# Attention over a sliding window of a cache, with both projections: the first weight chunks 4 and 5 as two loads, and V of unit 30 as one

## The chip, the cores and the metric

The kernel runs on one core of a Trainium2 chip. The metric is the time of one execution on the device in microseconds (us). TensorE (PE in the profile) does the matmuls and transposes, with its weight loads shown apart as PEld; VectorE is DVE, ScalarE is ACT, GpSimd is POOL, and SyncE (SP) issues the DMA transfers.

## What is computed

Eight sequences of 32 new tokens each (256 rows) are projected to queries of 32 heads, attend over the last 2048 positions of a given cache of K and V with 4 heads, each shared by 8 query heads, and are projected back.

```python
def reference(x, k_cache, v_cache, wq, wo):
    B, Sq, D = x.shape                      # 8, 32, 1024
    Hq, Dh = 32, 128
    Hkv, Sk = k_cache.shape[1], k_cache.shape[2]   # 4, 8192
    W = min(4096, max(256, Sk // 4))        # 2048
    rep = Hq // Hkv                         # 8
    q = (x @ wq).reshape(B, Sq, Hq, Dh).transpose(0, 2, 1, 3)
    k = jnp.repeat(k_cache[:, :, Sk - W:, :], rep, axis=1)
    v = jnp.repeat(v_cache[:, :, Sk - W:, :], rep, axis=1)
    scores = jnp.einsum("bhqd,bhkd->bhqk", q, k) * (Dh ** -0.5)
    p = softmax(scores)
    o = jnp.einsum("bhqk,bhkd->bhqd", p, v)
    return o.transpose(0, 2, 1, 3).reshape(B, Sq, Hq * Dh) @ wo
```

All data are bf16; sums are kept in fp32.

## The kernel before

The work is cut into 32 **units**, one for each pair of a sequence and a K/V head; units 0 to 7 belong to head group 0, and so on. A unit has 2048 keys in 16 tiles of 128, and 256 columns of queries (8 heads of 32 tokens). `run` walks through the units in four slots each. A slot computes the scores of four key tiles on TensorE (L504), has ScalarE take their exponential (L506), and issues, two slots late, the product with V (L515). V is first copied into a buffer `va` with a column of ones beside it (`va_copy`, L437 and L439), so that the product also gives the sum of the exponentials; `finish_unit` divides by it (L445 to L451).

The scores want K with its 128 channels on the partitions, and it comes there in three ways. Units 0, 1 and 2 are loaded plain and transposed on TensorE (L397 for unit 0, L244 for 1 and 2). Units 4, 7, 9 and some later ones are loaded plain, transposed in blocks on VectorE (L259) and moved into place by VectorE and GpSimd (L268, L270). All others are transposed by the DMA itself, in two halves (L200).

The projection of the queries is done by group: a group's part of Wq has 1024 columns, and its 1024 rows come as eight **chunks** of 128 (256 KB each), numbered 0 to 7. For group 0 this is done in `start`, before the first scores: for each chunk, eight matmuls (L405), one for each head. Ahead of chunk 6 stand the eight transposes of the first half of unit 0's K (`k_turn(0)`), after chunk 7 those of the second half. Then the query sums are cast (`q_copy`, L411) and the first scores follow. The later groups' queries (L285) and the output projection (L322) are spread over the slots of the attention by a plan written out by hand.

Nearly all loads are issued by SP, in the order in which the code calls them, and no engine changes its order of work at run time. In `start` this order is: the first half of x (the second is issued by ScalarE), the chunks of Wq up to 5, the first half of K of unit 0, chunks 6 and 7, the second half of that K, V of unit 0 and K of unit 1, and then V of unit 1 and K of units 2 and 4, V of unit 2 and unit 3. `load_wq` takes a tuple `cuts` that says how many chunks each load of a half holds. In this kernel chunks 4 and 5 are one load. Each half has one buffer, whichever way it is cut.

`load_v` brings a unit's V in one load of 512 KB, or in two of 256 KB where the unit's number is at least `V_HALVES`. A unit's `va_copy` reads the whole of it in one instruction either way.

A load tells of its landing through one of eight semaphores that all loads take in turn, whichever engine issues them. A load waits, before it is issued, for the landing of the one that had its semaphore last, which is the load eight places earlier. Loads wait for a free buffer too, where theirs was in use.

Of the kernel before, what the change touches and what calls it, by code (L numbers as in the profile page):

```python
# [17 lines left out]
RL_MIN = 1.0e-10  # L18
N_WARM = 8
VA_ROW = 160  # L20
V_HALVES = 30

PE_T = (0, 1, 2)

# [84 lines left out]
class Fast:  # L109
# [93 lines left out]
    def load_v(self, ui, eng):  # L203
        b, g = self.units[ui]
        self.v_sb[ui] = self.vp.tile([self.P, self.KT, self.Dh], BF16, name="v_sb", tag="v")
        n = self.KT // (2 if ui >= V_HALVES else 1)
        for j in range(0, self.KT, n):
# [131 lines left out]
    def start(self):  # L339
# [6 lines left out]

        nc.sync.dma_start(out=x_sb[:, 0, :], in_=xf[0:P, :])  # L347
        nc.scalar.dma_start(out=x_sb[:, 1, :], in_=xf[P:2 * P, :])
        wq0 = self.load_wq(0, 0, (1, 1, 1, 1)) + self.load_wq(0, 1, (2, 1, 1))
        for p in wq0[:5]:  # L350
            p()
        self.load_k(0, 0)
        wq0[5]()
        wq0[6]()
        self.load_k(0, 1)
        self.load_v(0, nc.sync)
        self.load_k(1)
# [336 lines left out]
```

## Time and profile before

| what | us |
|---|---|
| median of 6 runs | 184.62 (184.25 to 185.02) |
| the profiled execution: its time | 185.06 |
| the profiled execution: its span | 183.3 |
| TensorE busy in the span | 177.3 |
| ScalarE busy | 135.9 |
| VectorE busy | 126.5 |
| GpSimd busy | 89.1 |
| TensorE busy from 0 to 20 us | 17.65 |
| mean granted TensorE clock | 0.998 |

The span runs from the first to the last instruction of the program; the execution's time has some more around it. The page puts the span into 40 slices and gives each engine's busy share in tenths:

```profile
PE   7979999999999999999999999999999999999993
DVE  0218799689887699477799566777587987554253
ACT  2207889888798898898787787778787788888800
DMA  5999999899999999999899999999999989970013
```

A slice is 4.6 us. TensorE is full but for the first slices and the last. The DMA row is the mean busy share of the core's 16 DMA engines: it is full from the second slice until the last loads are in.

A row of instructions in time order gives the start, the length, the engine, the line of the code, the operation and what it writes and reads. SPq is SyncE's queue: such a row is the issue of a DMA, not its transfer, which goes on behind it; the time from issue to landing is given apart. An issue can be long because SP stands in it.

### The profile page before, as it was taken

What the parts mean: (1) busy time and instruction counts of PE and PEld (TensorE: products, weight loads), DVE (VectorE), ACT (ScalarE), POOL (GpSimd) and SP (SyncE); (2) the same over time, 40 slices, a digit from 0 to 9 for tenths busy, and PEclk for the clock granted to TensorE, in tenths of its full rate; (3) what the DMA queues carried; (4) which work ended last, traced back from release to release, by engine and by line L of the source; (5) the groups of instructions that cost most, each with busy time, mean ns of one, the idle gap of its engine ahead of it and who ended that gap; (6) DMA issues with size and microseconds to landing.
All of it is one profiled execution on the core that took longest, in us unless ns stands there. A gap on an engine that the chain in (4) does not pass through costs nothing.

```text
span 183.3 us, 5015 instructions
## 1 busy us (share of the span) xinstructions
PE 177.3 (97%) x2026; PEld 152.3 (83%) x2041; DVE 126.5 (69%) x257; ACT 135.9 (74%) x146; POOL 89.1 (49%) x138
## 2 busy tenths in 40 slices
PE   7979999999999999999999999999999999999993
PEld 2879999999999999997878899987778788888853
DVE  0218799689887699477799566777587987554253
ACT  2207889888798898898787787778787788888800
POOL 2003456059880695944938806929705949600000
PEclk9999999999999999999999999999999999999999
DMA  5999999899999999999899999999999989970013
GB/s 185 325 411 407 233 383 375 262 253 256 370 394 245 354 332 221 373 288 346 265 394 355 399 259 284 363 267 359 279 302 257 350 268 340 209 201 0 0 35 90
DMA packets 52954, 51.73 MB, mean 282 GB/s; under 512 B 39744, under 2 KB 40256, under 8 KB 52928
## 3 DMA queue, kind: packets, MB, share of 16 engines
q1 hardware_dynamic: 52352, 50.90, 98.3%
q10 hardware_dynamic: 576, 0.49, 0.9%
q8 instruction: 16, 0.26, 0.6%
q14 instruction: 10, 0.08, 0.1%
HBM read 41.42 MB, written 0.52 MB: 229 GB/s over the span
## 4 chain that ended last, share of the span: by engine, by line
PE 92%; DMA 4%; SPq 1%; issue 1%; DVE 0%
PE o_ps L515 32%; PE s_ps L504 31%; PE op_ps L322 14%; PE q_ps L285 11%; DMA wq_sb<-in_wq_dram 4%; PE q_ps L405 2%; PE ql_ps L301 1%; PE tp L244 1%; SPq L168 1%; PE kf_ps L397 0%; SPq L347 0%; DVE o_t L332 0%; PE cnt_ps L570 0%
## 5 line engine op out<-in xcount | busy, mean ns | idle before, releaser
L506 ACT ACTIVATE pT<-s_ps 128x1024 bf16<-128x1024 f32 x128 | 128.4, 1027 | 26.9 <-PE s_ps L504 26.7
L270 POOL TENSOR_SCALAR kTv<-kb 32x512 bf16<-32x512 bf16 x126 | 84.3, 669 | 51.8 <-DVE kb L259 33.7
L515 PE MATMUL o_ps<-va,pT 128*128 128x129 bf16 x1024 | 78.8, 220 | 0.1
L515 PEld LDWEIGHTS <-pT 128*128 128x128 bf16 x1024 | 68.5, 98 | 3.1
L504 PE MATMUL s_ps<-QT,kT 128*128 128x256 bf16 x336 | 50.4, 272 | 0.1
L504 PEld LDWEIGHTS <-kT 128*128 128x128 bf16 x336 | 31.9, 98 | 9.4
L322 PE MATMUL op_ps<-wo_sb,OT 128*128 128x512 bf16 (+2 forms) x129 | 32.8, 353 | 0.6
L259 DVE STREAM_TRANSPOSE kb<-k_raw 128x512 bf16<-128x512 bf16 x44 | 29.7, 691 | 0.9 <-DMA k_raw<-in_k_cache_dram 0.5
L285 PE MATMUL q_ps<-xT,wq_sb 128*128 128x256 bf16 x192 | 28.3, 273 | 0.0
L439 DVE COPY va<-v_sb 128x2048 bf16<-128x2048 bf16 x30 | 25.9, 863 | 1.5 <-DMA v_sb<-in_v_cache_dram 1.1
L504 PE MATMUL s_ps<-QT,kTv 128*128 128x256 bf16 x176 | 26.4, 272 | 0.1
L445 DVE RECIPROCAL RL_all<-o_ps 128x2 f32<-128x2 f32 x32 | 5.3, 166 | 26.9 <-PE o_ps L515 26.5
L268 DVE COPY kTv<-kb 32x512 bf16<-32x512 bf16 x50 | 22.7, 455 | 1.2
L504 PEld LDWEIGHTS <-kTv 128*128 128x128 bf16 x176 | 17.0, 98 | 6.1
L285 PEld LDWEIGHTS <-wq_sb 128*128 128x128 bf16 x192 | 16.9, 98 | 1.2
L451 DVE STREAM_TRANSPOSE OT<-o_sb 128x256 bf16<-128x256 bf16 x32 | 14.3, 445 | 1.1
L449 DVE TENSOR_TENSOR o_sb<-o_ps,RL_all 128x256 bf16<-128x256 f32 x32 | 13.6, 424 | 1.1
L322 PEld LDWEIGHTS <-OT 128*128 128x128 bf16 x144 | 11.4, 98 | 2.3 <-DVE OT L451 0.2
L437 POOL TENSOR_SCALAR va<-v_sb 128x2048 bf16<-128x2048 bf16 x2 | 3.8, 1898 | 17.6 <-DMA v_sb<-in_v_cache_dram 17.6
L405 PE MATMUL q_ps<-xT,wq_sb 128*128 128x256 bf16 (+1 forms) x64 | 5.9, 246 | 1.3 <-DMA wq_sb<-in_wq_dram 1.3
L288 ACT CAST QT<-q_ps 128x512 bf16<-128x512 f32 x12 | 7.0, 583 | 0.2 <-PE q_ps L285 0.2
L405 PEld LDWEIGHTS <-wq_sb 128*128 128x128 bf16 x64 | 5.0, 98 | 2.1 <-DMA wq_sb<-in_wq_dram 1.4
(35 smaller groups left out, 42.8 us busy)
## 6 DMA issues: line engine op xcount, KB each, us to landing
v_sb<-in_v_cache_dram SPq DMA_DIRECT2D x30, 512.0 KB, 6.7
wo_sb<-in_wo_dram SPq DMA_DIRECT2D x16, 512.0 KB, 6.6
wq_sb<-in_wq_dram SPq DMA_DIRECT2D x13, 512.0 KB, 6.6
k_raw<-in_k_cache_dram SPq DMA_DIRECT2D x13, 512.0 KB, 5.8
wq_sb<-in_wq_dram SPq DMA_DIRECT2D x6, 256.0 KB, 5.1
v_sb<-in_v_cache_dram SPq DMA_DIRECT2D x4, 256.0 KB, 5.2
kT<-in_k_cache_dram SPq DMA_TRANSPOSE x36, 7.0
k_raw<-in_k_cache_dram SPq DMA_DIRECT2D x2, 256.0 KB, 7.3
```

Of the source, the lines that this page charges most:

```text
L259: nc.vector.transpose(out=st["kb"][:, sl, :], in_=self.k_raw[ui][:, sl, :])
L268: nc.vector.tensor_copy(out=out, in_=in_)
L270: nc.gpsimd.tensor_scalar(out=out, in0=in_, scalar1=1.0, scalar2=1.0, op0=ALU.mult, op1=ALU.mult)
L285: nc.tensor.matmul(st[k][:, hl % 2, :], lhsT=self.wq_t[g, i][:, c % (DC // 2), hl * P:(hl + 1) * P], rhs=self.xT[:, c, :], start=(c == 0 a ...
L322: nc.tensor.matmul(ps[:, 0:w], lhsT=self.OT[:, gq, c, t * P:(t + 1) * P], rhs=self.wo_t[gq][:, c, n0:n0 + w], start=(k == 0), stop=(k == 7))
L405: nc.tensor.matmul(ps, lhsT=self.wq_t[0, c // H][:, c % H, h * P:(h + 1) * P], rhs=self.xT[:, c, 0:n], start=(c == 0 and h in (0, 2, 4)), ...
L439: self.nc.vector.tensor_copy(out=out, in_=in_)
L449: nc.vector.tensor_tensor(out=o_sb[:, :, :, :], in0=o_ps[:, :, 0:Dh].rearrange("p q (i c) -> p q c i", c=4), in1=rl[:, ui * QT_N:(ui + 1) ...
L451: nc.vector.transpose(out=self.OT[:, g * QT_N:(g + 1) * QT_N, :, b * self.Sq:(b + 1) * self.Sq], in_=o_sb[:, :, :, :])
L504: nc.tensor.matmul(s_ps[:, jj, :], lhsT=self.kT[ui][:, c * CJ + jj, :], rhs=q_u, start=True, stop=True)
L506: nc.scalar.activation(out=pT[:, :, :], in_=s_ps[:, :, :], func=ACT.Exp, bias=0.0, scale=self.scale)
L515: nc.tensor.matmul(o_ps[:, qt, 0:self.VW], lhsT=pT[:, jj, qt * P:(qt + 1) * P], rhs=va[:, j, 0:self.VW], start=(j == 0 and qt == 0), stop= ...
```

## The change

Two edits. The second half of group 0's Wq is cut into four loads instead of three: chunks 4 and 5 come as two loads of 256 KB each. The list `wq0` has eight loads then, of which six are issued ahead of K's first half and two behind it; the order of the data is the same as before. And `V_HALVES` goes from 30 to 31, so that V of unit 30 is one load and only unit 31's V is split. In all, the number of loads stays the same, with one more between those two places.

```diff
-V_HALVES = 30
+V_HALVES = 31
...
-        wq0 = self.load_wq(0, 0, (1, 1, 1, 1)) + self.load_wq(0, 1, (2, 1, 1))
-        for p in wq0[:5]:
+        wq0 = self.load_wq(0, 0, (1, 1, 1, 1)) + self.load_wq(0, 1, (1, 1, 1, 1))
+        for p in wq0[:6]:
             p()
         self.load_k(0, 0)
-        wq0[5]()
         wq0[6]()
+        wq0[7]()
         self.load_k(0, 1)
```

The instructions of TensorE, VectorE, ScalarE and GpSimd and their order are the same in both programs; only SP's list differs.

## The prediction

> **What bounds the kernel now.** I read the page's busy shares first, then its chain, then the engine that they name: every wait of TensorE, then the head of the chain in order of time.
>
> ```profile
> PE 177.3 (97%) x2026; PEld 152.3 (83%) x2041; DVE 126.5 (69%) x257; ACT 135.9 (74%) x146; POOL 89.1 (49%) x138
> PE 92%; DMA 4%; SPq 1%; issue 1%; DVE 0%
> PE q_ps L405 <- DMA wq_sb<-in_wq_dram: 1.3, 1, 1.3
> PE warm_ps L375 <- PEq L678: 0.8, 1, 0.8
> PE xT_ps L383 <- DMA x_sb<-in_x_dram: 0.3, 1, 0.3
> ```
>
> The first two lines are of the page, the other three are all that the view of TensorE's waits has. TensorE is the bound: it is on 92% of the chain. The same view from 14 us on is empty, so after the head TensorE waits for no one; its one wait of size is for a Wq load, which is the 4% of DMA in the chain. The head of the chain (start, length, what; all in us):
>
> ```profile
> 3.08 7.18 DMA wq_sb<-in_wq_dram
> 10.26 0.05 issue
> 10.30 1.49 PE q_ps L405 x16
> 11.80 0.45 PE kf_ps L397 x8
> 12.24 1.32 PE q_ps L405 x16
> 13.56 0.45 PE kf_ps L397 x8
> 14.01 0.50 PE s_ps L504 x4
> ```
>
> The load issued at 3.08 is the joint one of chunks 4 and 5. It lands at 10.26. TensorE, done with chunk 3 at 9.04, stands until 10.30 (idle 1.27), then runs without a gap: chunks 4 and 5 issue until 11.63, 8 transposes of K until 12.08, chunk 6 until 12.74, chunk 7 until 13.40, 8 transposes, and the first scores at 13.92. (The chain counts by ends, these are starts of the single matmuls; one chunk takes 0.67 to the next one's start: 10.30 to 10.97 for the first of the two.)
>
> Last, SP's own row, because every load here stands in its queue (start, length, line, op, what, count):
>
> ```profile
> 0.75 0.39 SPq L347 DMA_DIRECT2D x_sb<-in_x_dram  x1
> 1.19 2.33 SPq L168 DMA_DIRECT2D wq_sb<-in_wq_dram  x5
> 3.57 0.47 SPq L197 DMA_DIRECT2D k_raw<-in_k_cache_dram  x1
> 4.78 0.87 SPq L168 DMA_DIRECT2D wq_sb<-in_wq_dram  x2
> 5.70 0.67 SPq L192 DMA_DIRECT2D k_raw<-in_k_cache_dram  x1
> 6.41 0.65 SPq L208 DMA_DIRECT2D v_sb<-in_v_cache_dram  x1
> 7.10 0.53 SPq L197 DMA_DIRECT2D k_raw<-in_k_cache_dram  x1
> 8.17 0.33 SPq L208 DMA_DIRECT2D v_sb<-in_v_cache_dram  x1
> 10.27 1.01 SPq L197 DMA_DIRECT2D k_raw<-in_k_cache_dram  x2
> ```
>
> Issue plus time to landing gives each load's landing: x 4.58 and 4.76; chunks 0 to 3 at 5.32, 5.98, 6.70, 8.16; chunks 4 with 5 at 10.26; K's first half 10.94; chunk 6 11.60; chunk 7 12.29; K's second half 12.96; V of unit 0 14.24. Two things are to be seen. From 10.26 on the landings are 0.66 to 0.69 apart for 256 KB and 1.28 for 512 KB, though the issues lie 0.4 to 1.2 apart: the loads arrive in order and at the pace of their bytes, and DMA is busy throughout (share 0.85 to 1.08 in every microsecond from 2 to 14). And SP stops where eight loads are in flight: chunk 6, the ninth with x's second half, is issued at 4.78, after x's first half has landed.
>
> **The change, part by part.**
>
> *One more load, at the fifth place.* Chunk 5 gets its own issue: the five of the row take 2.33, 0.47 each with the gap, so it goes out at 3.55. Its landing count is a 4-byte packet per DMA engine; in the trace the next data packet starts 15 ns behind such a packet, so all that follows lands 0.015 later. Bytes and their order stay.
>
> *When chunk 4 lands.* No row shows it. Below: 0.66 after chunk 3, 8.82. Above: one chunk's pace ahead of 10.26, 9.59. One DMA engine of the 16 trails then (the others end chunks 4 and 5 by 9.57), and its slow packets lie before 9.5, so I take the late end. It doesn't matter: at 9.59 chunk 4 starts at 9.63 (0.04 from landing to first matmul, as at 10.26 to 10.30) and is done when chunk 5 lands.
>
> *TensorE with the new landings* (each start is the later of engine free and landing + 0.015 + 0.043):
> - chunk 5 at 10.32, where its first matmul stood at 10.97: 0.65 ahead
> - transposes at 11.00 (K 10.94 + 0.06; they take 0.45), before 11.63: 0.63 ahead
> - chunk 6 at 11.66 (11.60 + 0.06; the engine is free at 11.45), before 12.08: 0.42 ahead
> - chunk 7 at 12.35 (12.29 + 0.06; free at 12.33), before 12.74: 0.39 ahead
> - transposes at 13.02, before 13.40; the first scores, which wait for the casts of q behind chunk 7, at 13.53, before 13.92: 0.39 ahead.
>
> So 0.65 is won and 0.26 given back: what is late next is chunk 6's landing, then chunk 7's. Of the idle 1.27, 0.88 stays in pieces.
>
> *SP's waits move.* The two programs' instruction lists show eight landing semaphores taken in turn by all loads, each issue waiting for the load eight earlier. With one more load ahead, K's first half becomes the ninth and waits for x (4.58): issued at 4.62, not 3.57. Queued behind it are chunk 6 (now behind x's second half, at 5.13), chunk 7 (5.50), K's second half (behind chunk 1, 6.04), V of unit 0 (behind chunk 2, 6.74), K of unit 1 (behind chunk 3, 8.20, was 7.10) and V of unit 1 (behind chunk 4, 9.6, was 8.17). K of unit 2 waits for 10.26 in both, and from there each load waits for the same load as before. I cost these delays at nothing: the data packets of K's first half begin on the first engine at about 8.3, where that one has ended chunks 4 and 5, 3.7 after the new issue (x shows 1.3 from issue to first packets, 0.75 to 2.0); V of unit 1 has over 4 us to the 14 or so where its turn comes. If this cover is gone, see the slower rival.
>
> *V of unit 30 as one load.* One issue of 0.5 on SP less (1.00 for the two at 151.71). The whole lands where the second half did, 159.69; its copy reads both halves at once, at 163.0, so 3.3 us lie between. The transposed loads behind it, 160.55 and 161.43, have 6.5 us and more to their first scores. Worth nothing either way, by these spans. The number of loads is as before again, so the outputs at the end keep their semaphores.
>
> *What the 0.39 meets later.* Loads don't come earlier, so slack to them shrinks. V of unit 0: landed 14.24, copied from 14.66 to 15.34, first used 16.12 (then 15.73, copy free to start at 14.27). K of unit 1: landed 15.52, used 16.57. K of unit 2: 18.48 to 20.13. V of units 1 and 2 go through GpSimd copies that end 2.0 and 2.4 ahead of use. Transposed K: tightest is unit 5's second half, 38.09 to 39.23. One load is met: VectorE waits for unit 4's K already,
>
> ```profile
> DVE kb L259 <- DMA k_raw<-in_k_cache_dram: 0.5, 1, 0.5
> ```
>
> and will wait 0.9. Behind it VectorE has unit 0's finish and the K copy of unit 2 at 21.67, which could then start at 21.45 (the finish ends 21.47) and end at 22.14; its scores, 22.81 before, want it at 22.42. Behind that VectorE is full until 31.06, the last move of unit 4's K, used at 31.71, then 31.32. All fits; the nearest has 0.26 left. ScalarE's exponentials (1.02 each) start behind the scores and move with them.
>
> *A rule that speaks against it.* The Trainium skill, "DMA: Bandwidth & Descriptors", section "Rules for kernel authors", wants at least 1 MiB per DMA for bandwidth; its "Anatomy of one DMA — SWDGE (gpsimd) path" gives 2.0 us plus bytes over 436 GB/s each (for loads issued by GpSimd; these are SP's). Paid in line, a further load would bring chunk 7 2.0 later, at 14.3, and the first scores about 1.6 later (0.45 lay between chunk 7's landing and its use): 186.2. The landings here show no such term: two of 256 KB take 1.34 to 1.37, one of 512 KB 1.28, a difference under 0.1. I go by the row.
>
> **Sum.** Minus 0.39 on the path, nothing elsewhere. Against the profiled execution (span 183.3, time 185.06, so 1.76 outside the span): span 182.9, time 184.67. The median of the runs, 184.62, is 0.44 below that execution; from it, **184.23**. Bounds of this case: chunk 7's and K's landings are read to about 0.1, and one DMA engine may trail by some tenths at another place in another run; 184.0 to 184.5.
>
> **Rivals.**
> - *Slower: landing hangs on issue.* If the 7.4 from issue to landing of K's first half were a latency and not a queue, K would land at 12.00, the transposes move from 11.63 to 12.04, chunk 6 to 12.49, and the first scores to 14.33: 0.41 later, 185.03. It decides once K's first half lands after 11.59. For it: 6.8 to 7.4 repeat over four loads. Against: landings evenly 0.7 apart behind uneven issues. Chance 0.21, with whatever else makes the head later.
> - *No difference.* The stall of 1.27 holds the trailing engine's delay of this one execution; where chunks 4 and 5 land by 8.7 there is nothing to win (TensorE could be through chunk 3 at 8.73), and the 0.26 on VectorE may be less than it looks. 184.6. Against: the runs lie only 0.77 apart, and the profiled one at the slow end, so landing would be at 9.5 or later and the same 0.39 follows. 0.14.
> - *More.* If chunks 6 and 7 come closer together than the trailing engine allowed here, all 0.65 stays: 183.97. Against: they keep one engine's pace for 256 KB, 0.66. 0.10.
>
> **How the numbers follow.** The forecast's case has 0.55. A measurement tells about 0.2%, 0.37 us, from no change, so the forecast is hardly over it: I put 0.42 of its 0.55 on faster, 0.13 on same. Faster 0.42 + 0.10 = 0.52; same 0.13 + 0.14 = 0.27; slower 0.21. The range reaches to the slower rival's 185.03 and a little below the third's: 183.9 to 185.05; the likeliest case alone has 184.0 to 184.5.
>
> **What would show it.** Right: K's first half issued at 4.6; TensorE's wait at L405 in pieces of about 0.6, 0.2 and less, 0.88 in all; the first scores at 13.53; landings of chunk 6 and 7 within 0.1 of 11.6 and 12.3; VectorE's wait for unit 4's K 0.9; no TensorE wait after 14. Wrong: K's first half, chunk 6 or 7 landing 0.3 later, or a new TensorE wait between 20 and 40 us.

## The result and the profile after

| | before | after |
|---|---|---|
| median, us | 184.70 (74 runs) | 184.12 (37 runs) |
| ratio after / before | | 0.9972 (95%: 0.9963 to 0.9982) |
| profiled execution: its time / its span, us | 185.06 / 183.3 | 184.23 / 182.5 |

The change makes the kernel 0.28% faster, 0.52 us of 184.7, with 0.33 to 0.68 in the interval. The forecast was 0.39. One execution after took 1057.63 us, for a reason that isn't known; the ratio leaves it out.

Of the page of after, first the busy shares and the chain by engine, then all that the view of TensorE's waits has (us in total, times, longest):

```profile
PE 177.1 (97%) x2026; PEld 152.2 (83%) x2041; DVE 125.5 (69%) x257; ACT 136.0 (75%) x146; POOL 89.4 (49%) x138
PE 86%; DMA 10%; DVE 1%; issue 1%
PE warm_ps L375 <- PEq L678: 0.8, 1, 0.8
PE xT_ps L383 <- DMA x_sb<-in_x_dram: 0.3, 1, 0.3
PE q_ps L405 <- DMA wq_sb<-in_wq_dram: 0.3, 1, 0.3
```

TensorE's work is what it was; its wait for Wq has gone from 1.3 to 0.3. And DMA has 10% of the chain instead of 4%: to that below. TensorE in the head, in order of time (start, length, line, what, count, idle before):

```profile
5.70 0.82 PE L405 MATMUL q_ps<-xT,wq_sb 128*128 128x256 bf16 x8
6.84 3.47 PE L405 MATMUL q_ps<-xT,wq_sb 128*128 128x256 bf16 x40 [0.32 <-DMA wq_sb<-in_wq_dram]
10.16 0.61 PE L397 MATMUL kf_ps<-ident,k_raw 128*128 128x128 bf16 x8
10.81 1.50 PE L405 MATMUL q_ps<-xT,wq_sb 128*128 128x256 bf16 x16
12.14 0.61 PE L397 MATMUL kf_ps<-ident,k_raw 128*128 128x128 bf16 x8
12.66 0.60 PE L504 MATMUL s_ps<-QT,kT 128*128 128x256 bf16 x4
```

The 40 matmuls from 6.84 are chunks 1 to 5 without a gap that the profile counts: chunk 4 is worked on while chunk 5 lands. The 0.32 ahead of them is chunk 1, which landed late here (6.80; 5.98 before). The first scores stand at 12.66, 1.26 earlier than in the trace of before. Most of that is not the change's doing, as the next section shows. SP's row:

```profile
0.75 0.39 SPq L347 DMA_DIRECT2D x_sb<-in_x_dram  x1
1.20 2.79 SPq L168 DMA_DIRECT2D wq_sb<-in_wq_dram  x6
4.51 0.33 SPq L197 DMA_DIRECT2D k_raw<-in_k_cache_dram  x1
4.88 1.19 SPq L168 DMA_DIRECT2D wq_sb<-in_wq_dram  x2
6.82 0.33 SPq L192 DMA_DIRECT2D k_raw<-in_k_cache_dram  x1
7.45 0.33 SPq L208 DMA_DIRECT2D v_sb<-in_v_cache_dram  x1
```

K's first half is issued at 4.51, when the second half of x, the one that ScalarE issues, has landed (4.49), 0.94 later than before; it still lands 0.68 behind chunk 5 (10.10 and 9.42), as it did before (10.94 and 10.26). Landings follow the bytes, not the issues.

Last, the chain in time order, where it passes from the loads to TensorE, and VectorE's wait for unit 4's K from 14 to 60 us:

```profile
10.12 9.34 DMA k_raw<-in_k_cache_dram
19.46 0.02 issue
19.48 0.71 DVE kb L259
...
21.19 0.59 DVE kT L246
21.77 0.05 issue
21.82 0.61 PE s_ps L504 x4
DVE kb L259 <- DMA k_raw<-in_k_cache_dram: 1.5, 1, 1.5
```

With the head ahead, unit 4's K (landed 19.46) has become what sets the pace: VectorE stands 1.5 for it with unit 0's finish and unit 2's transposed K queued behind, and unit 2's scores come 4.73 behind unit 1's, where it was 4.45 before. So 0.27 of the head start is given back there.

### The profile page after: what moved, and what is told of

Its sections match the earlier page's. It is cut to its first block, busy times and chain, and to the rows that moved or that the text cites. A ratio compares the mean times of both kernels' runs of the same rounds, so it can differ in the third digit from the quotient of the medians.

```text
span 182.5 us, 5014 instructions
## 1 busy us (share of the span) xinstructions
PE 177.1 (97%) x2026; PEld 152.2 (83%) x2041; DVE 125.5 (69%) x257; ACT 136.0 (75%) x146; POOL 89.4 (49%) x138
## 4 chain that ended last, share of the span: by engine, by line
PE 86%; DMA 10%; DVE 1%; issue 1%
PE o_ps L515 30%; PE s_ps L504 29%; PE op_ps L322 14%; PE q_ps L285 11%; DMA k_raw<-in_k_cache_dram 8%; DMA x_sb<-in_x_dram 2%; PE ql_ps L301 0%; DVE kb L259 0%; DVE kT L246 0%; DVE OT L451 0%; DVE o_sb L449 0%; DVE o_t L332 0%; DVE RL_all L445 0%; PE cnt_ps L570 0%
## 5 line engine op out<-in xcount | busy, mean ns | idle before, releaser
L439 DVE COPY va<-v_sb 128x2048 bf16<-128x2048 bf16 x30 | 24.9, 830 | 1.4 <-DMA v_sb<-in_v_cache_dram 1.1
L285 PEld LDWEIGHTS <-wq_sb 128*128 128x128 bf16 x192 | 16.9, 98 | 1.2
L329 DVE TENSOR_TENSOR oacc<-op_ps,oacc 128x512 f32<-128x512 f32 x8 | 5.3, 662 | 2.0 <-PE op_ps L322 2.0
```

The source lines that it names most:

```text
L285: nc.tensor.matmul(st[k][:, hl % 2, :], lhsT=self.wq_t[g, i][:, c % (DC // 2), hl * P:(hl + 1) * P], rhs=self.xT[:, c, :], start=(c == 0 a ...
L439: self.nc.vector.tensor_copy(out=out, in_=in_)
```

## The experiments

Single traces differ much in the head, so one number is read from all of them: how long after chunk 7's landing the first scores stand. Chunk 7's landing says how fast the loads were in that execution; what lies behind it is the kernel's own. "Unit 1 to unit 2" is the time from unit 1's first scores to unit 2's, and "last landing to end" the time from the landing of the last output to the end of the span. These are read from one trace of each kernel, in us. The last column compares times: 37 executions of the change and 22 of each other kernel, with 43 to 75 of before.

| kernel | chunk 7 lands | first scores | between | unit 1 to unit 2 | last landing to end | ratio to before (95%) |
|---|---|---|---|---|---|---|
| before | 12.29 | 13.92 | 1.63 | 4.45 | 0.90 | |
| the change | 11.43 | 12.66 | 1.23 | 4.73 | 0.90 | 0.9972 (0.9963 to 0.9982) |
| V of unit 30 whole, alone | 11.64 | 13.27 | 1.63 | 4.45 | 0.95 | 1.0007 (0.9990 to 1.0025) |
| 4 and 5 apart, alone | 11.30 | 12.53 | 1.23 | 4.94 | 1.34 | 1.0003 (0.9986 to 1.0019) |
| 0 with 1, 4 and 5 apart | 10.92 | 12.63 | 1.71 | 4.69 | 0.89 | 0.9976 (0.9960 to 0.9992) |
| a small load more | 11.30 | 12.89 | 1.59 | 4.90 | 0.89 | 1.0001 (0.9984 to 1.0018) |
| V of unit 29 in two as well | 11.24 | 12.88 | 1.64 | 4.81 | 1.34 | 1.0018 (1.0006 to 1.0030) |
| 5 with 6 | 11.11 | 12.77 | 1.66 | 4.70 | 0.89 | 0.9986 (0.9970 to 1.0001) |
| change, unit 4's block later | 11.51 | 12.74 | 1.23 | 4.45 | 0.89 | 1.0010 (0.9992 to 1.0029) |
| 0 with 1, block later | 11.36 | 12.94 | 1.58 | 4.45 | 0.89 | 0.9985 (0.9969 to 1.0000) |
| change, V of unit 31 whole too | 11.80 | 13.03 | 1.23 | 4.69 | 0.95 | 0.9975 (0.9960 to 0.9990) |
| 4 with 5, 6 with 7 | 11.87 | 13.76 | 1.89 | 4.45 | 0.90 | 1.0026 (1.0010 to 1.0042) |

The theory of **arrival** says that the gain is chunk 4's matmuls beside chunk 5's landing, less what chunks 6 and 7 still wait for. Its rivals: SP's later issues, and the end of the kernel.

**V of unit 30 whole, alone.**

```diff
-V_HALVES = 30
+V_HALVES = 31
```

> Edit: V of unit 30 as one load, chunks 4 and 5 still joint. Theory of arrival (the gain is that chunk 4's matmuls run while chunk 5 lands): no difference, within 0.15 us of before. Rival (a part of the gain comes from the end of the kernel, one issue less there or other semaphores for the outputs): 0.1 to 0.3 us faster.

Measured: no difference. Nothing at the end comes from this edit by itself.

**Chunks 4 and 5 apart, alone.**

```diff
-        wq0 = self.load_wq(0, 0, (1, 1, 1, 1)) + self.load_wq(0, 1, (2, 1, 1))
-        for p in wq0[:5]:
+        wq0 = self.load_wq(0, 0, (1, 1, 1, 1)) + self.load_wq(0, 1, (1, 1, 1, 1))
+        for p in wq0[:6]:
...
-        wq0[5]()
         wq0[6]()
+        wq0[7]()
```

> Edit: chunks 4 and 5 as two loads, V of unit 30 still in two, so all loads behind are one semaphore further to the end. Theory of arrival: the whole gain, 0.4 to 0.5 us faster than before. Rival (both edits are needed, the outputs at the end wait for other loads): gain under 0.25 us.

Measured: no difference, 1.0003. The theory of arrival, alone, is wrong about this kernel. Its head has the gain (1.23 instead of 1.63), and its last matmul starts at 179.37, close to the change's 179.28. But from the last output's landing to the end it takes 1.34, where the others take about 0.9. The view of the end's line shows SP's waits there (engine, operation, count: shortest, median and longest in ns, first and last start; eight of the ten are those for the landings, two come later), first of the change, then of this kernel:

```profile
L689 SPq EVENT_SEMAPHORE  x10: 17/28/28, 180.2 to 182.4; - x10
```

```profile
L689 SPq EVENT_SEMAPHORE  x10: 17/28/28, 181.5 to 182.7; - x10
```

At the end SP waits for the eight landing semaphores one after another, in the order of their numbers. In the change the first waits are passed from 180.2 on, while the outputs are still under way (the last lands at 181.56). In this kernel the first wait is passed at 181.5, just behind the last landing at 181.45, and the other seven come behind it, at 181.54, 181.60, 181.67 and so on to 181.91, 0.06 to 0.07 apart. The reason is the semaphore of the last output. Outputs take the semaphores in turn with the loads, so one load more moves each of them on by one: in the traces the last output has number 7 in the change, the last to be waited for, and number 0, the first, in this kernel.

**Chunks 0 and 1 as one load, 4 and 5 apart.** As before, seven loads of weights, five of them ahead of K.

```diff
-        wq0 = self.load_wq(0, 0, (1, 1, 1, 1)) + self.load_wq(0, 1, (2, 1, 1))
+        wq0 = self.load_wq(0, 0, (2, 1, 1)) + self.load_wq(0, 1, (1, 1, 1, 1))
```

> Edit: chunks 0 and 1 as one load, chunks 4 and 5 as two. The number of loads ahead of K's first half is that of before, so no issue waits for another load than before; chunk 0 is there with chunk 1, at 5.98 us in the trace of before, and TensorE took it up at 6.09. Theory of arrival: the same gain as the change, 0.4 to 0.5 us faster than before. Rival (the gain comes from SP's issues being later, with fewer loads in flight, so that the trailing DMA engine trails less): no gain, within 0.15 us of before.

Measured: 0.9976, as the change, though no issue up to chunk 7's waits for another load than before (K's first half goes out at 3.60; it was 3.57). The four issues behind it do wait for a later chunk, which the expectation overlooked: K's second half goes out at 6.06 instead of 5.70, and still lands in its turn, 0.66 behind chunk 7. The view of TensorE's waits over the whole span has one line left:

```profile
PE warm_ps L375 <- PEq L678: 0.8, 1, 0.8
```

TensorE takes up the first chunk at about 6.1 and never stands again in the head; its 1.71 is its own work, and says nothing of the gain. So the gain needs none of the waits that the change adds on SP ahead of K's first half.

**A small load more, chunks 4 and 5 joint.** (`V_HALVES` is 31.)

```diff
...
         for p in wq0[:5]:
             p()
+        scr = self.c1.tile([P, 64], BF16, name="scr")
+        nc.sync.dma_start(out=scr[:, :], in_=xf[0:P, 0:64])
         self.load_k(0, 0)
```

> Edit: chunks 4 and 5 stay joint, a load of 16 KB of x into a tile that nobody reads goes ahead of K's first half, and V of unit 30 is one load: SP's waits are those of the change, without its cut. Theory of arrival: no gain, within 0.15 us of before (16 KB are 0.04 us at the pace of the other loads). Rival of later issues: 0.4 to 0.5 us faster. Rival that the later issues cost (landing hangs on issue): 0.3 to 0.4 us slower.

Measured: 1.0001, no difference. K's first half is issued at 4.42, as late as in the change, and lands at 9.95, in its turn. Later issues neither win nor cost anything that can be measured (0.30 us faster to 0.33 slower lie in the interval). The head's 1.59 says the same of a gain; the time alone might hide one, as this trace loses 0.54 at unit 7, which is told below.

**V of unit 29 in two as well**, on the kernel before: the semaphores of the end alone.

```diff
-V_HALVES = 30
+V_HALVES = 29
```

> Edit: before, with V of unit 29 in two loads as well, so chunks 4 and 5 stay joint and all loads and outputs behind unit 29 are one semaphore further, as in the run with the cut of chunks alone. Theory of the end (SP goes through the landing semaphores one by one in the order of their numbers, some 0.06 us each; if the last output has number 0, the seven others are gone through behind it): 0.35 to 0.45 us slower than before, all of it behind the last landing. Rival (the cut of chunks alone gains nothing for a reason at the head): no difference, within 0.15 us of before.

Measured: 1.0018, which is 0.33 us slower (0.11 to 0.55); again 1.34 from the last landing to the end. The end's 0.44 is shown apart from the head.

**Chunks 5 and 6 as the joint load.**

```diff
-        wq0 = self.load_wq(0, 0, (1, 1, 1, 1)) + self.load_wq(0, 1, (2, 1, 1))
-        for p in wq0[:5]:
+        wq0 = self.load_wq(0, 0, (1, 1, 1, 1)) + self.load_wq(0, 1, (1, 2, 1))
+        for p in wq0[:6]:
...
-        wq0[5]()
         wq0[6]()
```

> Edit: chunks 5 and 6 are the joint load, chunk 4 is alone, all three ahead of K's first half, chunk 7 behind it; seven loads of weights as before. Theory of arrival by the same sum: chunk 5 waits for chunk 6's bytes, 0.67 later than in the change, and K's transposes and chunks 6 and 7 follow without a gap, so the first scores stand where they stood before: no difference to before, within 0.15 us. Rival (that chunk 4 starts early is the gain, wherever the joint load lies): 0.3 to 0.5 us faster.

The trace has 1.66 between chunk 7's landing and the scores, the sum's 1.63 and a little. The times don't decide: 0.9986 (0.9970 to 1.0001), with no difference just inside the interval and the rival's 0.3 us too.

**Unit 4's first block one slot later**, on the change and on the kernel with chunks 0 and 1 joint.

```diff
-V_T = {4: (None, (4, 6, 6, 7), 8, 13, 8),
+V_T = {4: (None, (5, 6, 6, 7), 8, 13, 8),
```

> Edit: the change, with VectorE's first block of unit 4's K one slot later (5 for 4), behind unit 0's finish. Theory of what is given back (with the head ahead, VectorE waits for that K's landing and the transposed K of unit 2 comes late; the traces of three kernels with an early head lose 0.2 to 0.5 us between units 1 and 2): 0.15 to 0.35 us faster than the change, 0.6 to 0.85 faster than before. Rival (what is lost there comes back later, by loads that land in their own time): as the change, 0.4 to 0.55 faster than before.

> Edit: chunks 0 and 1 joint, 4 and 5 apart, V of unit 30 in two, and VectorE's first block of unit 4's K one slot later. Both theories as for the run before it, on a head that waits for no other loads than before: 0.6 to 0.85 us faster than before if what is given back at unit 2 stays won, 0.4 to 0.6 if it is lost later.

The theory was missed in both: 1.0010, no difference to before, and 0.9985, 0.28 us faster (0.00 to 0.57). The rival is missed too in the first; in the second its 0.4 lies in the interval. The loss at unit 2 is gone in both traces (4.45). But on the change more than that is lost at units 6 and 7: their first scores stand 5.51 and 6.38 behind those of the unit before, 5.31 each in the trace of before. VectorE's waits from 14 to 60 us in the first of the two, then TensorE's:

```profile
DVE va L439 <- DMA v_sb<-in_v_cache_dram: 1.6, 1, 1.6
```

```profile
PE s_ps L504 <- POOL kTv L270: 0.4, 1, 0.4
PE s_ps L504 <- DMA kT<-in_k_cache_dram: 0.3, 1, 0.3
```

V of unit 5 landed at 37.34 there (35.55 in the change), VectorE stood for it with unit 7's last block behind, and GpSimd's moves of unit 7's K ended late. The kernel with the small load shows the same (V of unit 5 at 37.30, unit 7's scores 5.85 behind unit 6's). In these two traces a 16 KB packet of the instruction queue starts at 35.23 (block later) and 33.94 (small load), 2.1 and 3.4 before that landing; in the others it starts from 35.32 to 36.07, beside landings from 35.52 to 35.89. Whether it is the cause was not tried. In the trace with chunks 0 and 1 joint nothing is lost at units 6 and 7; why its times are no better than without the later block (0.9976) stays open (the intervals overlap). In that execution TensorE stood 1.3 for the joint load of chunks 0 and 1.

**V of unit 31 whole too**, on the change: the last output has number 6.

```diff
-V_HALVES = 31
+V_HALVES = 32
```

> Edit: the change, with V of unit 31 as one load too: one load fewer than before and than the change, so the last output has semaphore number 6 instead of 7. Theory of the end (one more semaphore is gone through behind the last landing, some 0.06 us): as the change within 0.15 us, 0.4 to 0.6 us faster than before. Rival (the way V of the last units is cut matters in itself): 0.3 us or more away from the change, as the run with the cut of chunks alone was.

Measured: 0.9975, as the change; 0.95 at the end instead of 0.90. It isn't V of unit 30 that counts, but the number of loads.

**Two joint loads**, 4 with 5 and 6 with 7, and `V_HALVES` 29 to keep the number of loads.

```diff
-        wq0 = self.load_wq(0, 0, (1, 1, 1, 1)) + self.load_wq(0, 1, (2, 1, 1))
+        wq0 = self.load_wq(0, 0, (1, 1, 1, 1)) + self.load_wq(0, 1, (2, 2))
...
-        wq0[6]()
```

> Edit: chunks 4 with 5 and 6 with 7 are two joint loads of 512 KB, V of unit 29 comes in two so that the number of loads stays. Theory of arrival by the same sum: chunk 6 waits for chunk 7's landing, 2.03 us behind that of chunk 5, where TensorE wanted it 1.82 behind: chunks 6 and 7 and the first scores 0.27 us later, 0.2 to 0.35 us slower than before. Rival (a load more or less is worth nothing at the head, only the landings' order): no difference, within 0.15 us of before.

Measured: 1.0026, 0.48 us slower (0.18 to 0.78), and in the trace 1.89, which is 0.26 over before where the sum gave 0.27. TensorE's waits for Wq over the whole span, and its head:

```profile
PE q_ps L404 <- DMA wq_sb<-in_wq_dram: 1.5, 2, 1.2
```

```profile
9.89 1.49 PE L404 MATMUL q_ps<-xT,wq_sb 128*128 128x256 bf16 x16 [1.19 <-DMA wq_sb<-in_wq_dram]
11.22 0.61 PE L396 MATMUL kf_ps<-ident,k_raw 128*128 128x128 bf16 x8
11.91 1.49 PE L404 MATMUL q_ps<-xT,wq_sb 128*128 128x256 bf16 x16
13.24 0.61 PE L396 MATMUL kf_ps<-ident,k_raw 128*128 128x128 bf16 x8
```

After the transposes' issue (11.22 and 0.45) TensorE is free at 11.67, and chunk 6, which it could have had, starts at 11.91 with chunk 7.

No version was faster than the change beyond what the measurement tells; the ones with chunks 0 and 1 joint and with V of unit 31 whole are level with it.

## Why the prediction was right, point by point

- **The sum at the head held.** From chunk 7's landing to the first scores it had 12.29 to 13.92 before and, with 0.015 more on the landing, 12.31 to 13.53 after: 1.63 and 1.22. The traces have 1.63 and 1.23, and 1.23 again in the three other kernels with the plain cut. That the landings of chunks 6 and 7 are late next is so too: chunk 6 lands at 10.76 and starts at 10.81; chunk 7 lands at 11.43 and starts at 11.48, which is also when TensorE is through with chunk 6.
- **Chunk 4 one pace ahead of chunk 5**: 8.74 and 9.42, 0.68 apart. Chunks 6 and 7 keep that pace, 0.66 apart, so the rival in which they come closer together falls.
- **The size** came out at 0.52, the forecast's 0.39 within the interval's 0.33 to 0.68. That single traces put the first scores 1.26 apart is mostly the loads of these two executions: chunk 7 landed 0.86 earlier in that of after. So the times that were forecast from the start (first scores at 13.53, chunks 6 and 7 within 0.1 of 11.6 and 12.3) were missed, and only the distances held. Over twelve traces chunk 7 landed from 10.92 to 12.29, and the kernels with 4 and 5 joint reach down to 11.24, so it isn't shown that the change makes the loads faster. Whether more than 0.40 is won stays open.
- **The rival of no difference** was put aside because chunks 4 and 5 would land at 9.5 or later in every execution. That is not so. In the other three traces with this joint load and chunks 6 and 7 apart they landed at 9.61, 9.23 and 9.22, and TensorE stood 1.02, 0.50 and 0.22 for them, where it was 1.27 in the trace of before. An execution can't win more at the head than TensorE stands there, so the last could have won 0.22 at most. How often that happens isn't known.
- **SP's later issues at nothing**: right. In the change K's first half is issued 0.94 later and lands as far behind chunk 5 as before, and the kernel with the small load shows no cost beyond 0.33. The slower rival, landing by issue, falls with it. One reading was wrong, without consequence: the ninth load waits for the half of x that ScalarE issues, which lands last (4.76 before, 4.49 after), not for the other (4.58 and 4.33).
- **V of unit 30 "worth nothing either way"** is the step that failed. The slack of 3.3 us behind its landing was read rightly, and alone it is worth nothing. But with the cut of the chunks it decides all: without it the last output's semaphore has number 0, and the end takes 0.44 longer, which eats the gain. The prediction did note that the outputs keep their semaphores, and did not ask what it would cost if they didn't. Had the change been the cut alone, the forecast would have been wrong by its whole size.
- **What the gain meets later**: the place was right, unit 2's K behind the wait for unit 4's. The forecast left 0.26 of room behind its 0.39; where an execution is further ahead, the room is used up and the rest is given back there (0.24 to 0.49 in the seven traces with first scores by 13.03 and unit 4's block in its old place). The wait came to 1.5 instead of 0.9 for the same reason.
- **Idle of TensorE in the head** was to be 0.88 in pieces, the largest ahead of chunk 5; it was 0.36, of which 0.32 ahead of chunk 1 and 0.04 ahead of chunk 6. The pieces depend on how far one DMA engine trails in an execution, which the prediction took from one trace: in that of after, chunk 1 was there on fifteen engines by 6.20 and on the last at 6.80.
- **The estimate of 186.2**, in which a further load costs a time of its own in line, had the wrong sign; the pace of the landings in the trace gave the right one. In the change chunks 4 and 5 land 0.68 apart as two loads.

## What to carry to other kernels

Where TensorE waits for a load at the head of a kernel, cut it at the granularity in which it is consumed, and carry each new landing through the following steps: the gain ends where the next landing paces. When loads take a small set of semaphores in turn, count them to the end of the program: a load more or less anywhere moves the last output to another semaphore, and the end of this program walks through them in a fixed order. And compare the distance from a landing to its user rather than times from the start, when the loads of single executions differ by more than the change is worth.

## What was not expected of the hardware

The end of the kernel: SP goes through eight landing semaphores in the order of their numbers, 0.06 to 0.07 us each, even when all have been reached; with the last output on the first number this put 0.44 us behind the last landing (1.34 instead of 0.90, in both kernels that have it so), and 0.05 more than in before with the output on the last but one (0.95). And the pace of the first loads: the landing of the same chunk, with some 2.7 MB loaded by then, spread over 1.4 us between executions. A part of it is one DMA engine that trails: chunk 7 was there on fifteen engines by 11.61 and on the last at 12.29 in the trace of before, by 10.89 and at 10.92 in the fastest. Why the fifteen differ as well isn't shown.
